# RWKV attention feeding a routed expert layer: the first chunks reordered, an early table and some weight splits moved

## The chip, the cores and the metric

The kernel runs on one core of a Trainium2 chip. The metric is the device time of one execution in microseconds (us), as the median of several runs. The core has five engines that each work through their own instructions in order: TensorE (PE, with its weight loads as PEld), VectorE (DVE), ScalarE (ACT), GpSimd (POOL) and SyncE (SP). SP here only issues transfers; ACT and POOL issue some as well. PE has two clock levels, 1.2 and 2.4 GHz; the profile gives the granted clock as a share of the higher one.

## The reference

Two stages follow each other. The first is a linear attention with a decaying state, for 4 batches, 8 heads, 768 positions and a head size of 48; the second sends each of the 3072 rows of its result to one of 8 experts.

```python
for t in range(S):
    kt, vt, rt = k[:, :, t], v[:, :, t], r[:, :, t]
    cur = np.einsum('bhd,bhe->bhde', u[None] * kt, vt)
    y[:, :, t] = np.einsum('bhd,bhde->bhe', rt, state + cur)
    state = w[None, :, :, None] * state + np.einsum('bhd,bhe->bhde', kt, vt)
...
logits = x @ w_gate                      # x: the attention's result, 3072 x 384
expert_idx = np.argmax(logits, axis=1)   # gate_w: softmax weight of that expert
...
h = np.maximum(np.einsum('ecd,edf->ecf', disp, w1), 0.0)   # 384 -> 1024
y = np.einsum('ecf,efd->ecd', h, w2)                       # 1024 -> 384
out[i] = gate_w[i] * y[expert_idx[i], pos[i]]
```

Each expert takes the rows sent to it in order, up to a capacity.

## The kernel before

**Chunks.** The attention is cut into 24 chunks of 128 positions (`NI`, six per batch). Chunk `i` reads four tensors: `dm` (r and k with the head dimension on partitions, 393 KB), `bd` (r, k and v compact per half chunk, 590 KB), and, unless it is the last of its batch, `tk` and `tv` (k and v rows, 197 KB each); together 1.38 MB. All are issued by SP, in `load` (L485) and `load_v` (L503). `dm`, `tk` and `tv` have three buffers each and `bd` has four, so a load waits until the chunk three or four back has been used.

**Work of a chunk.** POOL forms the bonus products r*u*k from `bd` and the table `ubt`, which holds u on all 128 partitions (`bonus`, L512 and L513). DVE sums them (`reduce_bonus`, L561). ACT writes the sums on diagonals of two score tiles `s0` and `s1` (`diag`, L520 and L521, eight instructions) and copies v into block form (`blocks`, L527). DVE scales r and k by powers of the decay (`prep_keys`, L537 and L545) and k rows by `kk` (`prep_values`, L554). PE multiplies these to scores (`scores`, L568 and L571). DVE and ACT lay the scores over the diagonals through the mask `msk` (`masks`, L580 to L582). PE forms the state's update (`update`, L592; DVE L600 and L602 add and scale it) and the chunk's values (`values`, L613, L614, L617). ACT copies them to `x` (L619, two buffers) and issues the store to DRAM (L620). One chunk later PE turns `x` round (`xpose`, L80; ACT copies it to `xt`, L82) and forms its eight logits (`logits`, L91; ACT L92 reads them out of the same PSUM tile that the next `xpose` takes).

**Order.** The order on every engine is the order of the source; nothing is rearranged. Ahead of the loop (L626 to L663) the first chunks are loaded and prepared: chunk 2 entirely, with its sum of the bonus, before the loop begins. In the loop, iteration `i` issues on PE: scores of chunk i+1, the transposition of x of i-1, the update of i, routing matmuls (`step`, L105), the values of i, the logits of i-1. `diag` of chunk i+2 stands after the values in iterations 0 and 1 and before them later. Preparation of chunk i+3 (`prep`) ends the iteration.

**Routing.** `route` (L110) is a generator that `step` advances by a stage: DVE finds the best expert, PE ranks the rows (L136, L137, into a PSUM tile with the tag `lg`, one buffer), DVE compares the ranks with a ramp, and PE adds the rows' numbers into a table (L180) which DVE accumulates in `acc` (L181). In iteration 20 the table is read a first time for expert 0 (`table`, L261: four transpositions into a tile with the tag `lg`, three DVE instructions). It is read for all experts after the last chunk's routing, and the rows are then gathered by indirect transfers of POOL (`gather`, L275).

**Weights.** `wstream` (L233) loads expert weights in pieces (SP, L239) and splits each of 14 halves into a high part (ACT, L247) and a low part (DVE, L248). `PLAN0` places the fetches and splits of expert 0 in the loop's iterations. After the loop `layer1(0, f)` for f = 0 to 7 runs the first layer of expert 0's early rows; the last chunk's routing is interleaved with it (L713 to L738).

**Start of the kernel.** POOL builds constants (the identity, `rev`, `eye`, the mask as float `mf`), DVE the powers of the decay (`setup1`), and PE runs matmuls on zeros (`warm`) so as to be busy. `ubt` is loaded by two broadcast transfers (L492). `setup3` (L446) builds the routing's constants on POOL.

## Time and profile before

| | us |
|---|---|
| median of three runs | 435.44 |
| lowest and highest | 433.3 and 436.03 |
| the profiled execution, whole | 437.47 |
| its span, first to last instruction | 435.7 |

| engine | busy us | share of the span |
|---|---|---|
| PE | 414.2 | 95% |
| DVE | 273.9 | 63% |
| POOL | 235.2 | 54% |
| ACT | 228.9 | 53% |

The mean granted clock of PE was 0.964. The attention takes the first 173 us or so; the experts take the rest. The shares are averages over stages with different limits, so each stage is read for itself. "Busy" of PE counts a matmul at the lower clock as twice as long, so a PE that is busy all the time may still be working at half its speed. A line "A <- B" of the waits says that A stood idle until B released it.

### The profile page before, as it was taken

The page shows a single profiled execution, that of the slowest core. Times are in us where ns is not written, and L with a number is a line of the kernel's source. Part 1 is how long each engine was busy: PE and PEld are TensorE (multiplying, and loading weights), DVE is VectorE, ACT ScalarE, POOL GpSimd, SP SyncE. Part 2 cuts the span into 40 slices and gives each one's busy share as a digit, 9 for nine tenths or more (in the row PEclk, how much of TensorE's full clock was granted, in tenths as well). Part 3 has the DMA queues.
Part 4 walks back from the last instruction along what each step waited for, and adds up shares of the span by engine and source line. Part 5 has one row for each costly group of instructions (what it writes and reads, how often), then busy time and mean ns, then how long its engine had stood idle before and what let it go on. Part 6 is the DMA issues. An engine that isn't in the chain of part 4 may idle for free.

```text
span 435.7 us, 8123 instructions
## 1 busy us (share of the span) xinstructions
PE 414.2 (95%) x2911; PEld 402.6 (92%) x2912; DVE 273.9 (63%) x595; ACT 228.9 (53%) x607; POOL 235.2 (54%) x242
## 2 busy tenths in 40 slices
PE   7789999999999799999999999999999999999993
PEld 3678999999999798899999999999999999999992
DVE  5696879999999957676355365464563554644310
ACT  6755787777778545354346265273472552742401
POOL 5985148387846351158886384682882540620703
PEclk9686999999999989699999999999999999999998
DMA  7996997789689113326736456566565553430112
GB/s 221 300 296 206 342 296 247 251 274 297 221 259 327 38 57 108 129 68 153 189 75 170 142 119 161 138 155 171 122 157 160 163 149 126 116 85 5 25 33 65
DMA packets 52963, 72.07 MB, mean 165 GB/s; under 512 B 29654, under 2 KB 38312, under 8 KB 52912
## 3 DMA queue, kind: packets, MB, share of 16 engines
q1 hardware_dynamic: 20528, 56.84, 42.5%
q0 software_dynamic: 28928, 9.89, 10.9%
q10 hardware_dynamic: 3456, 4.72, 3.0%
q8 instruction: 25, 0.41, 0.4%
q14 instruction: 26, 0.21, 0.2%
HBM read 62.06 MB, written 9.79 MB: 165 GB/s over the span
## 4 chain that ended last, share of the span: by engine, by line
PE 75%; DMA 8%; DVE 5%; issue 4%; POOL 3%; ACT 2%; SPq 1%; POOLq 0%; ACTq 0%; DVEq 0%
PE a L304 8%; PE a L305 8%; PE a L306 8%; PE b L323 7%; PE b L325 7%; PE b L324 7%; PE y L613 4%; PE y L614 4%; PE a L568 4%; PE y L617 4%; PE a L571 4%; DMA xg<-x_dr,idsc 3%; PE xp L91 3%; PE u L592 3%; PE yp L339 2%
## 5 line engine op out<-in xcount | busy, mean ns | idle before, releaser
L331 POOL DMA_INDIRECT out<-yo,idsc x28 | 59.3, 2116 | 63.0 <-ACT yo L330 56.6
L278 POOL DMA_INDIRECT xg<-x_dr,idsc x28 | 60.3, 2152 | 42.9 <-PE tp L287 35.9
L304 PE MATMUL a<-xh,ws 128*128 128x412 f32 (+2 forms) x216 | 76.7, 355 | 0.4 <-DVE hl L310 0.4
L309 ACT ACTIVATE hh<-a 128x412 fp32r<-128x412 f32 (+2 forms) x72 | 35.1, 487 | 74.8 <-PE a L306 74.5
L305 PE MATMUL a<-xl,ws 128*128 128x412 f32 (+2 forms) x216 | 73.3, 339 | 0.1
L306 PE MATMUL a<-xh,ws 128*128 128x412 f32 (+2 forms) x216 | 73.0, 338 | 0.0
L323 PE MATMUL b<-hh,ws 128*128 128x412 f32 (+2 forms) x216 | 72.8, 337 | 0.0
L324 PE MATMUL b<-hl,ws 128*128 128x412 f32 (+2 forms) x216 | 71.3, 330 | 0.0
L325 PE MATMUL b<-hh,ws 128*128 128x412 f32 (+2 forms) x216 | 71.3, 330 | 0.0
L310 DVE SCALAR_TENSOR_TENSOR hl<-a,hh 128x412 fp32r<-128x412 f32 (+2 forms) x72 | 39.5, 551 | 49.2 <-ACT hh L309 48.9
L248 DVE TENSOR_TENSOR ws<-wr,ws 128x384 fp32r<-128x384 f32 (+1 forms) x112 | 66.4, 612 | 3.7 <-ACT ws L247 3.6
L247 ACT CAST ws<-wr 128x384 fp32r<-128x384 f32 (+1 forms) x112 | 59.3, 557 | 0.1
L326 DVE COPY yt<-b 128x412 f32<-128x412 f32 (+2 forms) x27 | 14.5, 539 | 68.0 <-PE b L325 68.0
L304 PEld LDWEIGHTS a<-xh,ws 128*128 128x128 f32 x216 | 41.7, 193 | 1.0 <-DVE hl L310 0.6
L305 PEld LDWEIGHTS a<-xl,ws 128*128 128x128 f32 x216 | 41.7, 193 | 0.8 <-DVE xl L292 0.6
L306 PEld LDWEIGHTS a<-xh,ws 128*128 128x128 f32 x216 | 41.6, 192 | 0.1
L291 ACT CAST xh<-tp 128x412 fp32r<-128x412 f32 (+2 forms) x27 | 12.5, 478 | 54.1 <-PE tp L287 54.1
L324 PEld LDWEIGHTS b<-hl,ws 128*128 128x128 f32 x216 | 40.7, 189 | 0.1
L323 PEld LDWEIGHTS b<-hh,ws 128*128 128x128 f32 x216 | 40.7, 189 | 0.1
L325 PEld LDWEIGHTS b<-hh,ws 128*128 128x128 f32 x216 | 40.5, 188 | 0.1
L512 POOL TENSOR_TENSOR t<-bd,ubt 128x384 f32<-128x384 f32 x24 | 30.3, 1264 | 17.7 <-DMA bd<-bdc 11.9
L520 ACT ACTIVATE s<-eye,bon 128x64 f32<-128x64 f32 x96 | 32.4, 338 | 13.7 <-DVE bon L561 7.6
(191 smaller groups left out, 864.1 us busy)
## 6 DMA issues: line engine op xcount, KB each, us to landing
bd<-bdc SPq DMA_DIRECT2D x23, 576.0 KB, 5.6
wr<-w SPq DMA_DIRECT2D x24, 512.0 KB, 6.6
wr<-w SPq DMA_DIRECT2D x32, 384.0 KB, 7.2
dm<-dmj SPq DMA_DIRECT2D x24, 384.0 KB, 4.5
x_dr<-x ACTq DMA_DIRECT2D x24, 192.0 KB, 3.3
tk<-rkv SPq DMA_DIRECT2D x20, 192.0 KB, 5.7
tv<-rkv SPq DMA_DIRECT2D x20, 192.0 KB, 5.8
xg<-x_dr,idsc POOLq DMA_INDIRECT x28, 12.9
```

Of the source, the lines that this page charges most:

```text
L247: nc.scalar.copy(out=hi, in_=r)
L248: nc.vector.tensor_tensor(out=lo, in0=r, in1=hi.bitcast(F32), op=ALU.subtract)
L278: nc.gpsimd.indirect_dma_start(out=xg[k % 2][:q, i], out_offset=None, in_=x_dr[:n, :], in_offset=bass.IndirectOffsetOnAxis(ap=ids[k][:q, i ...
L304: nc.tensor.matmul(a, lhsT=wh, rhs=xh[:, d, :n], start=d == 0, stop=False)
L305: nc.tensor.matmul(a, lhsT=wh, rhs=xl[:, d, :n], start=False, stop=False)
L306: nc.tensor.matmul(a, lhsT=wl, rhs=xh[:, d, :n], start=False, stop=d == 2)
L309: nc.scalar.activation(hh[:, f, :n], a, AF.Relu)
L310: nc.vector.scalar_tensor_tensor(out=hl[:, f, :n], in0=a, scalar=0.0, in1=hh[:, f, :n].bitcast(F32), op0=ALU.max, op1=ALU.subtract)
L323: nc.tensor.matmul(o, lhsT=wh, rhs=hh[:, f, :n], start=f == 0, stop=False)
L324: nc.tensor.matmul(o, lhsT=wh, rhs=hl[:, f, :n], start=False, stop=False)
L325: nc.tensor.matmul(o, lhsT=wl, rhs=hh[:, f, :n], start=False, stop=f == 7)
L331: r = nc.gpsimd.indirect_dma_start(out=out[:, :], out_offset=bass.IndirectOffsetOnAxis(ap=ids[k][:qo, i, 0:1], axis=0), in_=yo, in_offset= ...
```

## The change

- **Loads.** `us` (u in two rows, 3 KB) replaces the two broadcasts into `ubt`: POOL builds a 2 x 128 matrix `half` of zeros and ones, PE multiplies it with `us`, ACT copies the result to `ubt`. Chunk 0's first part of `bd` is issued before `dm`; `bd`'s v part and `tv` of chunk 0 come before chunk 1; chunk 3 and `tv` of chunks 1 and 2 are issued before the work on chunk 0.
- **Masks and constants.** `msk` and the memset of `snb[0]` go ahead of the bonus products on POOL. `setup3` is split: its first part stands before the bonus of chunk 3, the rest (`setup4`) after the values of chunk 1. The zeroing of `vdb[2]` on ACT goes behind the masks of chunk 0.
- **Warm matmuls.** 8 in place of 10 at the start; 6 before the scores of chunk 0 in place of 3 after the transpositions of `setup1`. The matmul and copy of `setup_keys` go ahead of the scores of chunk 0.
- **Bonus sums.** Up to chunk 4 the sum is taken by itself: for chunks 2, 3 and 4 behind the values of chunks 0, 1 and 2, directly ahead of their `diag` (which for chunk 4 moves from before to after the values). `prep_values` of chunk 2 also moves there.
- **Stores.** The stores of x for chunks 0, 1 and 2 are issued by SP, not ACT.
- **Early table.** In iteration 20 the routing step and the values come before the table of expert 0, not behind it.
- **Splits.** Splits 11, 12 and 13 of expert 0 leave iterations 22 and 23 and follow `layer1(0, 2)`, `(0, 3)` and `(0, 4)`.

The diff, its core:

```diff
-SPLIT0 = {..., 21: (6, 7, 8), 22: (9, 10, 11), 23: (12, 13)}
-PLAN0 = [((FETCH0[i],) if i in FETCH0 else (), SPLIT0.get(i, ())) for i in range(NI)]
+SPLIT0 = {..., 21: (6, 7, 8), 22: (9, 10)}
+PLAN0 = [((FETCH0[i],) if i in FETCH0 else (), SPLIT0.get(i, ())) for i in range(NI)] + [((), (n,)) for n in range(11, 14)]
...
+            us = sup.tile([2, DM], F32, name="us")
+            half = sup.tile([2, 128], F32, name="half")
+            nc.sync.dma_start(out=us, in_=ub)
             make_identity(nc, idn)
+            nc.gpsimd.memset(half, 1.0)
+            nc.gpsimd.affine_select(out=half, in_=half, ...)
+            nc.gpsimd.affine_select(out=half, in_=half, ...)
...
-            warm(10)
+            warm(8)
+            up = ps1.tile([128, DM], F32, tag="lg", name="up")
+            nc.tensor.matmul(up, lhsT=half, rhs=us, start=True, stop=True)
...
+            nc.scalar.copy(out=ubt.rearrange("p a b d -> p (a b d)"), in_=up)
             setup2()
+            nc.gpsimd.tensor_copy(out=msk, in_=mf)
             for a in (rtb[1], kdb[1]):
                 nc.gpsimd.memset(a[96:], 0.0)
+            nc.gpsimd.memset(snb[0], 0.0)
...
-                if "bon" not in t:
+                if i > 4:
                     reduce_bonus(i)
...
-                nc.scalar.dma_start(out=x_dr[C * i:C * i + C, :], in_=x)
+                (nc.sync if i < 3 else nc.scalar).dma_start(out=x_dr[C * i:C * i + C, :], in_=x)
...
             load(0)
-            load(1)
             nc.sync.dma_start(out=T[0]["bd"][:, 2], in_=bdc[0, 0, :, 2])
             load_v(0)
+            load(1)
             load(2)
+            load_v(1)
+            load(3)
+            load_v(2)
             bonus(0)
...
             w128, oki, g = setup1(sup, ps1)
+            setup_keys(ps1, g)()
+            warm(6)
             prep_keys(0)
             scores(0)
-            keys = setup_keys(ps1, g)
+            blocks(0)
             reduce_bonus(0)
+            prep_values(0)
+            prep_keys(1)
             diag(0)
-            keys()
+            masks(0)
+            nc.scalar.copy(out=vdb[2].rearrange("p a e -> p (a e)"), in_=zc.broadcast_to([128, 768]))
             setup_state(sup, w128, oki)
-            blocks(0)
-            prep_keys(1)
-            masks(0)
-            prep_values(0)
             prep_values(1)
+            reduce_bonus(1)
             diag(1)
             blocks(1)
-            load_v(1)
-            load(3)
             bonus(2)
...
-            prep(2)
+            setup3()
             bonus(3)
-            setup3()
+            prep_keys(2)
...
             for i in range(NI):
-                each(load_v, i + 2)
+                if i != 1:
+                    each(load_v, max(i + 2, 3))
...
                 update(i)
+                if i < NI - 1:
+                    step()
+                if i > 2:
+                    each(diag, i + 2)
+                values(i)
                 if i == 20:
                     ids[0] = table("a", 0, PASSES[0][2], range(1), ("lg", 1))[:, 0]
-                if i < NI - 1:
-                    step()
-                if i > 1:
-                    each(diag, i + 2)
-                values(i)
                 if i == NI - 1:
                     step()
-                if i <= 1:
+                if i == 0:
+                    prep_values(2)
+                if i <= 2:
+                    reduce_bonus(i + 2)
                     diag(i + 2)
                 each(blocks, i + 2)
                 scale(i)
                 step()
+                if i == 1:
+                    setup4()
...
             for f in range(2, 5):
                 layer1(0, f)()
+                next(ws)
```

## Rows read from the trace of the kernel before

**Rows 1.** The page's 40 equal slices of the span, in tenths.
```profile
PEclk9686999999999989699999999999999999999998
```

**Rows 2.** Busy time by stretch: start:end, length, engines, granted clock, DMA share, GB/s.
```profile
10.00:15.00 5.00, 1.05 (x5) 1.08 (x6) 3.53 (x8) 3.14 (x12) 4.73 (x8) 0.71 1.05 315
...
30.00:35.00 5.00, 3.91 (x19) 3.67 (x19) 4.72 (x7) 3.37 (x12) 2.96 (x4) 0.50 1.03 305
```

**Rows 3.** The critical chain, 0 to 75 us: start, length, what.
```profile
3.00 5.99 DMA bd<-bdc
...
15.68 8.70 DMA dm<-dmj
...
24.46 0.38 ACTq L620
...
24.89 0.35 ACT s L520
...
26.91 0.40 ACT vd L527
...
41.23 0.99 PE a L568 x8
...
43.08 0.33 PE xp L80 x3
...
45.88 0.89 PE y L617 x8
46.77 0.60 PE xp L91 x6
47.37 0.99 PE a L568 x8
```

**Rows 4.** Waits from 5 to 41 us: total us, times, longest.
```profile
DVE bon L561 <- POOL t L513: 6.3, 3, 3.4
ACT s L520 <- DMA dm<-dmj: 5.8, 2, 3.6
...
PE xp L91 <- ACT xt L82: 1.6, 1, 1.6
```

**Rows 5.** Timeline of the first 30 us: start, length, instruction.
```profile
9.16 1.01 POOL L512 TENSOR_TENSOR t<-bd,ubt 128x384 f32<-128x384 f32 x1 [4.29 <-DMA bd<-bdc]
...
11.99 0.68 DVE L537 TENSOR_TENSOR rt<-dm,ft 96x512 f32<-96x512 f32 x1
...
12.59 1.22 DVE L545 TENSOR_TENSOR kd<-dm,kb 96x1024 f32<-96x1024 f32 x1
...
13.95 2.05 PE L568 MATMUL a<-rt,kd 128*128 128x128 f32 x8 [3.96 <-POOL msk L635]
...
20.59 1.08 PE L568 MATMUL a<-rt,kd 128*128 128x128 f32 x8
...
24.13 2.01 DVE L545 TENSOR_TENSOR kd<-dm,kb 96x1024 f32<-96x1024 f32 x1
...
29.57 2.06 PE L568 MATMUL a<-rt,kd 128*128 128x128 f32 x8
```

**Rows 6.** Timeline around iteration 20, 148 to 159 us.
```profile
151.06 0.18 PE L136 MATMUL rk<-oh,tri 128*128 128x16 bf16 x1 [2.56 <-DVE idsa L272]
...
158.21 0.44 DVE L581 COPY_PREDICATED s1b<-msk,a 128x256 f32<-128x256 int32 x1 [3.26 <-PE a L571]
```

**Rows 7.** Timeline after the last chunk, 174 to 187 us.
```profile
174.28 0.93 ACT L247 CAST ws<-wr 128x384 fp32r<-128x384 f32 x2
...
175.10 1.03 DVE L248 TENSOR_TENSOR ws<-wr,ws 128x384 fp32r<-128x384 f32 x2
...
186.91 0.42 DVE L310 SCALAR_TENSOR_TENSOR hl<-a,hh 128x256 fp32r<-128x256 f32 x1 [1.16 <-ACT hh L309]
```

**Rows 8.** Transfers issued from 0 to 50 us: count, KB each, median us to landing.
```profile
x_dr<-x ACTq DMA_DIRECT2D x4, 192.0 KB, 6.2
...
ubt<-ub SPq DMA_DIRECT2D x2, 96.0 KB, 4.5
```

More of the change, by code (lines that the diff above doesn't have):

```diff
@@ L31 @@
 FETCH0 = {3: 0, 4: 1, 9: 2, 13: 3, 16: 4, 18: 5, 19: 6}
[L32 to L33 removed]
+SPLIT0 = {7: (0,), 8: (1,), 10: (2,), 13: (3,), 15: (4,), 16: (5,), 21: (6, 7, 8), 22: (9, 10)}
+PLAN0 = [((FETCH0[i],) if i in FETCH0 else (), SPLIT0.get(i, ())) for i in range(NI)] + [((), (n,)) for n in range(11, 14)]
 GROUPS = [(0, 4), (4, 4), (8, 4), (12, 4), (16, 2), (18, 2), (20, 2), (22, 2)]
@@ L376, in rwkv_moe @@
             nc.sync.dma_start(out=wt, in_=wv)
+            us = sup.tile([2, DM], F32, name="us")
+            half = sup.tile([2, 128], F32, name="half")
+            nc.sync.dma_start(out=us, in_=ub)
             make_identity(nc, idn)
+            nc.gpsimd.memset(half, 1.0)
+            nc.gpsimd.affine_select(out=half, in_=half, compare_op=ALU.is_ge, fill=0.0, base=0,
+                                    pattern=[[1, 128]], channel_multiplier=-64)
+            nc.gpsimd.affine_select(out=half, in_=half, compare_op=ALU.is_ge, fill=0.0, base=63,
+                                    pattern=[[-1, 128]], channel_multiplier=64)
             nc.gpsimd.memset(hm, 1.0)
@@ L418, in setup1 @@
                 nc.scalar.copy(out=g, in_=gp)
-                nc.scalar.copy(out=vdb[2].rearrange("p a e -> p (a e)"), in_=zc.broadcast_to([128, 768]))
-                warm(3)
                 return sq[7], oki, g
@@ L452, in setup3, with setup4 @@
                 start(0)
+            def setup4():
                 nc.gpsimd.iota(ramp, pattern=[[1, WL]], base=0, channel_multiplier=0, allow_small_or_imprecise_dtypes=True)
@@ L487, in load @@
                 t = T[i] = {}
-                dm = t["dm"] = ld.tile([96, 2, NP, 128], F32, tag="dm", name=f"dm{i}", bufs=3)
-                nc.sync.dma_start(out=dm, in_=dmj[b, c])
-                if i == 0:
-                    for h in range(2):
-                        nc.sync.dma_start(out=ubt[64 * h:64 * h + 64].rearrange("p a b d -> p (a b d)"),
-                                          in_=ub[h:h + 1].broadcast_to([64, NP * 2 * D]))
                 bd = t["bd"] = ld.tile([128, 3, 8, D], F32, tag="bd", name=f"bd{i}", bufs=4)
@@ L496, in load @@
                     nc.sync.dma_start(out=bd[:, 0:2], in_=bdc[b, c, :, 0:2])
-                else:
+                dm = t["dm"] = ld.tile([96, 2, NP, 128], F32, tag="dm", name=f"dm{i}", bufs=3)
+                nc.sync.dma_start(out=dm, in_=dmj[b, c])
+                if i:
                     nc.sync.dma_start(out=bd, in_=bdc[b, c])
@@ L633, in rwkv_moe @@
                 nc.gpsimd.memset(a[96:], 0.0)
-            nc.gpsimd.memset(snb[0], 0.0)
-            nc.gpsimd.tensor_copy(out=msk, in_=mf)
             bonus(1)
             w128, oki, g = setup1(sup, ps1)
+            setup_keys(ps1, g)()
+            warm(6)
             prep_keys(0)
             scores(0)
-            keys = setup_keys(ps1, g)
+            blocks(0)
             reduce_bonus(0)
+            prep_values(0)
+            prep_keys(1)
             diag(0)
-            keys()
+            masks(0)
+            nc.scalar.copy(out=vdb[2].rearrange("p a e -> p (a e)"), in_=zc.broadcast_to([128, 768]))
             setup_state(sup, w128, oki)
-            blocks(0)
-            prep_keys(1)
-            masks(0)
-            prep_values(0)
             prep_values(1)
+            reduce_bonus(1)
             diag(1)
             blocks(1)
-            load_v(1)
-            load(3)
             bonus(2)
```

1 line of the change is left out of this document (removed).

## The prediction

> **What bounds the kernel now.** I read the page's slices first. The granted clock is well below full in three places: slices 2 to 4, slice 15 and slice 17 [rows 1]; at 10.9 us a slice these are the stretch from 11 to 44 us, that from 152 and that from 174 us. Elsewhere PE runs at 2.4 GHz and is busy nearly all the time, so a gain is to be looked for in these three places, and the change touches all three.
>
> The critical chain comes next. From 41.23 us on it is PE, one loop iteration after another; iteration 3 lasts 47.37 − 41.23 = 6.14 us [rows 3]. Before that it is transfers and short steps of other engines: chunk 0's `bd` lands at 3.00 + 5.99 = 8.99 us [rows 3] and the bonus starts at 9.16 [rows 5]; a load of `dm` lands at 15.68 + 8.70 = 24.38 us and releases a store's issue on ACT [rows 3]. By the timeline, the scores that open iterations 0, 1 and 2 start at 13.95, 20.59 and 29.57 us [rows 5], those of iteration 3 at about 41.2 [rows 3]. So iterations 0 to 2 took 6.6, 9.0 and 11.6 us where 6.14 (4.3 for the first) would do. The windows say why a longer one costs twice: transfers run at 300 GB/s with all engines taken, and from 30 to 35 us PE gets half its clock [rows 2]; matmuls of L568 that take 1.08 us there take 2.06 [rows 5].
>
> The waits name what is late: DVE waited 6.3 us in three places for POOL's bonus, and with DVE's strict order the masks behind it waited too; ACT stood 5.8 us in two places before `diag` until a transfer landed, which was the issue of a store; PE waited 1.6 us for `xt` and 4.0 us for `msk` or the keys beside it [rows 4, 5].
>
> **The change, part by part: the head.** I rebuild the opening from rows.
>
> *Loads.* A chunk is 1.38 MB, at 300 GB/s 4.6 us, below the 6.14 us of an iteration; the head's transfers bind only because they start late and in the wrong order. The two `ubt` transfers (4.5 us to landing [rows 8]) become 3 KB, and `bd` has nothing ahead of it, so it lands 2 to 4 us before 8.99. POOL then sets the bonus's start: it gets `half` (three small instructions, some 0.7 us), `msk` and a memset (0.6 and 0.5) ahead of it and was free at 9.16 − 4.29 = 4.9 us, hence about 6.8 us against 9.16 [rows 5]. With two instructions of 1.01 us and DVE's sum the first `diag` starts near 9.5. By bytes ahead of it, `dm` of chunk 1 lands at about 10 us, of chunk 2 at 13.8, of chunk 3 at 18.4, of chunk 4 at 23.
>
> *Iteration 0.* Keys take 0.68 + 1.22 us of DVE [rows 5], so the scores of chunk 1 start at about 12.2, not 13.95. The six warm matmuls and `gq` delay the scores of chunk 0 to about 10.3; they end at 12.2, just in time. `diag` takes 26.91 − 24.89 = 2.0 us [rows 3] and ends at 12.5, two masks at 13.4, ahead of the values at 14.7. PE's work of iteration 0 is 6.14 − 0.33 − 0.89 − 0.60 = 4.3 us (no transposition, no state, no logits [rows 3]): it ends at 16.6, and the keys of chunk 2 (13.8 + 1.9, behind chunk 1's sum) are ready at 16.3.
>
> *Iteration 1.* 6.14 us, and a wait: `xt` of chunk 0 stands on ACT behind `diag` and `blocks` of chunk 2, 3 us that start when POOL's bonus is summed, at 19.0; the logits wait 0.8 us. It ends at 23.6.
>
> *Iteration 2.* The next `xpose` needs the logits read out by ACT, behind `diag` and `blocks` of chunk 3: with DVE's sum at 24.4 this is 27.5 us, and PE, through its scores at 25.5, waits 2.0 us. It ends at 31.8. *Iteration 3* has this wait once more, as `diag` of chunk 4 now follows the values: 3.1 us of ACT plus a copy against 2.5 us of PE, 1.2 us. It ends at 31.8 + 6.14 + 1.2 = 39.1 us, against 47.37 [rows 3]: 8.3 us gained at the full clock with nobody in anybody's way.
>
> Two deductions. DVE and POOL slow each other: the keys' instruction takes 1.22 us, and 2.01 when POOL works beside it [rows 5]. Iterations 0 to 2 hold three of these and some smaller ones; bounds 0 and 4 us, I take 1.5. And PE still has gaps ahead of 12 us. In the profile a gap of 3.96 us [rows 5] stands just before the clock falls, so one stretch at 1.2 GHz is likely; it doubled 1.08 us to 2.06. Bounds 0 (no fall) and 5 us (a whole iteration, 11.6 − 6.14, as iteration 2 was); I take 1.8. **The head gives 8.3 − 1.5 − 1.8 = 5.0 us**, bounds 0 and 8.3.
>
> *Stores by SP.* ACT no longer holds still for the store's turn (5.8 us [rows 4]); this gain is in the sum already. Behind each store on SP stand the later loads: of `dm`, `bd` and `tk` for chunks 6 and 7 and `tv` of chunk 4. They wait for buffers until about then anyway, and are used two iterations later. The Trainium skill speaks against this part: in "DMA: Bandwidth & Descriptors", section "Issuing engines are not separate DMA queues", it says that transfers run on the same 16 engines whoever starts them, and that a choice of issuer only saves the sequencer's time. By that rule two moved issues give 2 x 0.38 us. The rows show more than issue time at stake on ACT, since what is behind the issue waits as well; that the landing gets no earlier is a rival below.
>
> *Covered.* `setup4` (some 1.7 us of POOL) goes behind chunk 1's values, under POOL's idle time between bonuses; uncovered it delays one bonus by 1.7 us. The zeroing of `vdb[2]` (0.8 us of ACT) stands where ACT waits for the sum of chunk 1. The `up` matmul runs in place of two warm ones; its copy delays `kb` by 0.5 us, under the wait for `dm`.
>
> **The early table.** In iteration 20 the rank matmul waits 2.56 us, as the table's tile has the same tag and is read by DVE behind two state updates [rows 6]. PE then falls to 1.2 GHz for a while (slice 15 [rows 1]). Afterwards the rank needs no such read, and the values (1.8 + 0.89 us [rows 3]) run while DVE works off its backlog; table and DVE reads meet about 3 us later with nothing behind them. PE gains up to 2.6 us of waiting and about 1.7 us of half clock. DVE limits this: it then waited 3.26 us for the scores of chunk 22 [rows 6], and the masks behind them can move up by no more than that. I take 3.0, bounds 0 and 4.
>
> **The splits.** Splits 12 and 13 are 0.93 us of ACT and 1.03 us of DVE, between the last logits and the operands of `layer1(0, 0)` [rows 7]; without them these come about 0.5 us sooner. Afterwards three splits, 1.5 us of DVE, stand among `layer1`, where DVE had one idle piece of 1.16 us [rows 7]; the rest, 0.4, delays the accumulation for the last table. Two weight fetches wait for their buffers some 8 us longer, still ahead of their own splits. Net 0.5, bounds −0.5 and 3.5, the last if PE's fall to 1.2 GHz at about 176 us (slice 17 [rows 1]) goes too.
>
> **Sum.** 5.0 + 3.0 + 0.5 = 8.5 us. The profiled execution took 437.47 us (span 435.7), two more than the median of 435.44; from the median it is 435.44 − 8.5 = 427 us.
>
> **Rivals.**
>
> *PE keeps its full clock.* Then the head gives near its 8.3, the table 3 to 4 and the end 2 to 3: about 14 us, 421 us. For it: the new warm matmuls bridge the gap before chunk 0's scores. Against it: waits for ACT of 1 to 2 us remain in iterations 1 to 3.
>
> *The head stays slow.* ACT, DVE and POOL are near full there (POOL 4.73 of 5 us in one window [rows 2]), and if each iteration again ends in a wait that costs the clock, the head gains 0 to 1 us. With table and splits: 435.44 − 4 = 431.5 us.
>
> *The table's move does nothing.* If DVE, not the tile, holds iteration 20, the wait reappears at the next masks. Then 435.44 − 5.5 = 430 us.
>
> *The stores hold `x`; slower.* `x` has two buffers, so the copy of chunk 2's values waits until chunk 0's store has landed. By the rule above SP makes that no sooner: the median is 6.2 us [rows 8], and with loads ahead of it on the queue I put it at 31 us, just when the copy is ready. Each us later holds ACT, with `diag` of chunk 4 and the logits' copy behind it, and so PE; the stores of chunks 1 and 2 may repeat it. It takes 8.5 us in all to eat the gain and 13 to be slower by over 1%, three holds of over 4 us: with two of 6.2 and one of 1.5 about 441 us.
>
> **How the numbers follow.** The forecast, 424 to 429.5 us, gets 0.52; full clock 0.20; no table 0.10; slow head 0.12; stores 0.06. About 1% (4.4 us) is what a measurement of this kernel tells from no change: faster means below 431.1. Forecast, full clock, 0.06 of the no-table case and 0.02 of the slow head are faster, 0.80; the rest of these two, 0.14, the same; the stores 0.06, slower. The range from 420.5 to 432 leaves out the stores and the ends of the two outer cases.
>
> **What would show it.** In the new profile: the loads of `dm` for chunk 1 landing near 10 us; scores starting at about 12, 17, 24 and 33 us; no wait of ACT's `diag` for a transfer; iteration 20 without a wait of the rank for the table, and no fall of the clock at its place. Wrong would be: ACT's copy of `x` (L619) waiting for a transfer, DVE's keys at 2 us each, or slices of the clock below 8 tenths beyond the fourth.

## The result, and the profile after

The changed kernel takes 430.82 us as the median of 18 runs (427.8 to 433.56); the kernel before takes 435.94 us beside it (431.8 to 440.76, 18 runs). That is 5.1 us less by the medians; the ratio is 0.9915 [0.9887, 0.9943], a gain of 3.7 us. A ratio leaves out executions that lie over 1.5% above the fastest of their kernel and a median does not, so the two differ, by up to 2.4 us in the table of the experiments; I compare parts by medians on the same chip and give the ratio where it says something else. The forecast of 427.0 us was too low by 3.8: sign and range held, the size did not, and by the ratio the change lies just inside the 1% that I had given 0.14.

The page of the changed kernel, its span, its engines and the granted clock in 40 slices:

```profile
span 428.3 us, 8132 instructions
...
PE 408.5 (95%) x2914; PEld 394.9 (92%) x2915; DVE 275.0 (64%) x595; ACT 229.3 (54%) x608; POOL 237.0 (55%) x245
...
PEclk9998999999999999999999999999999999999998
```

Of the three places where the clock was low [rows 1], the ones at iteration 20 and at the start of the first layer are gone, and one slice of the head is left, at 8 tenths (the first slice deceives, see the head below). The two profiled executions stand 437.47 − 430.09 = 7.4 us apart, more than the medians, since that of before lay 1.5 us above its median. The trace splits the 7.4 by events on PE: the scores of chunk 7 start at 58.80 before and 57.32 after, 1.5 us of **head**; iteration 20, from the scores of chunk 21 to those of chunk 22, lasts 156.10 − 145.16 = 10.94 us before and 150.27 − 143.68 = 6.59 after, 4.35 us of **table**; from chunk 22 to the second layer's first matmul it is 34.81 us before and 32.87 after, 1.9 us at the **end**, where the splits are (the rest of the span gives 0.4 back). So between these two profiles the table gave more than forecast, the end more, and the head, the largest term, far less.

**Iteration 20.** Timeline of the kernel after, 146 to 153 us (start, length, instruction, idle time before and its releaser):

```profile
146.60 0.17 PE L136 MATMUL rk<-oh,tri 128*128 128x16 bf16 x1
...
149.38 0.42 PE L267 MATMUL tba<-idn,acc 72*64 72x72 f32 x4
...
150.27 1.14 PE L577 MATMUL a<-rt,kd 128*128 128x128 f32 x8
...
152.98 0.42 DVE L590 COPY_PREDICATED s1b<-msk,a 128x256 f32<-128x256 int32 x1
```

The rank no longer waits [rows 6 has 2.56 us], the table's transpositions follow without a wait, and the masks of chunk 22 stand 5.2 us sooner, with no wait of DVE ahead of them.

**The head.** Opening scores of each chunk on PE, in us; the forecast is that of the steps ahead of their deductions.

| chunk | forecast | before | after | after, a second profile (`e14_again`) | the same head alone (`e1_head`) |
|---|---|---|---|---|---|
| 1 | 12.2 | 13.95 | 14.82 | 13.89 | 14.94 |
| 2 | 16.6 | 20.59 | 19.83 | 18.47 | 19.84 |
| 3 | 23.6 | 29.57 | 27.70 | 28.12 | 27.70 |
| 4 | 31.8 | 41.08 | 38.01 | 36.13 | 36.41 |
| 5 | 39.1 | 47.22 | 45.68 | 43.81 | 44.09 |

Already the first row is wrong: chunk 1 came hardly sooner than before, or later. Timeline of the kernel after, 4 to 34 us:

```profile
7.10 1.51 POOL L521 TENSOR_TENSOR t<-bd,ubt 128x384 f32<-128x384 f32 x1 [0.46 <-ACT ubt L488]
8.69 1.32 POOL L522 TENSOR_TENSOR t<-t,bd 128x384 f32<-128x384 f32 x1
...
7.85 2.71 DVE L550 TENSOR_TENSOR kd<-dm,kb 96x512 f32<-96x512 f32 x2
10.49 0.54 DVE L570 TENSOR_REDUCE bon<-t 128x8 f32<-128x384 f32 x1
...
12.37 2.02 DVE L554 TENSOR_TENSOR kd<-dm,kb 96x1024 f32<-96x1024 f32 x1
...
10.53 2.70 PE L477 MATMUL warm<-oob 128*128 128x512 bf16 x6
13.07 1.05 PE L577 MATMUL a<-rt,kd 128*128 128x128 f32 x8
...
27.01 0.83 PE L91 MATMUL xp<-wgs,xt 128*128 128x8 f32 x6 [1.43 <-ACT xt L82]
...
32.02 0.55 PE L80 MATMUL xp<-idn,x 128*128 128x128 f32 x3 [2.32 <-ACT l L92]
```

The bonus starts at 7.10 (6.8 forecast) instead of 9.16 [rows 5]. What sets chunk 1's scores is PE itself: it goes without a break from the six warm matmuls to the scores of chunk 0, at 13.07 and not at 10.3 us, and from these to the scores of chunk 1. The warm matmuls run at 1.2 GHz and take 2.70 us; in `e15_stores`, at 2.4 GHz, the same six take 1.46 (timeline of that run, 8 to 12 us):

```profile
8.96 1.46 PE L478 MATMUL warm<-oob 128*128 128x512 bf16 x6
```

The clock record of the changed kernel's profile begins with the rise at 13.03 us, and views print full clock for what lies ahead of the first record; the 9 of its first slice and the 1.00 of the window from 10 us below are no evidence against these durations.

A second limit lies close behind. DVE now forms the keys while POOL forms the bonus: chunk 0's take 2.71 us (1.28 before), POOL's two products 1.51 and 1.32 instead of 1.01 and 0.99, and chunk 1's keys take 2.02 instead of 1.22, ending at 14.39, 0.4 us ahead of the scores that use them. Chunk 2's keys, 2.01 us, end at 17.67 + 2.01 = 19.68, just before its scores at 19.83. What ACT costs later is as forecast: the waits of PE from 5 to 46 us (us in total, times, longest) have 3.6 us for the logits' read where I had 2.0 + 1.2.

```profile
POOL t L521 <- DMA bd<-bdc: 3.9, 4, 1.7
...
PE xp L80 <- ACT l L92: 3.6, 2, 2.3
...
ACT s L529 <- DVE bon L570: 3.4, 2, 1.9
...
PE xp L91 <- ACT xt L82: 1.4, 1, 1.4
```

No line of ACT waiting for a transfer is left [rows 4 has 5.8 us]. The windows (start:end, length, busy time of PE, PEld, DVE, ACT, POOL, granted clock, DMA share, GB/s) show one fall of the clock after the first rise, from 33.5 to 36.9 us, behind PE's wait of 2.32 us, in the stretch that [rows 2] shows at 0.50:

```profile
10.00:15.00 5.00, 5.00 (x26) 3.07 (x25) 4.12 (x5) 3.42 (x11) 4.35 (x5) 1.00 1.01 318
30.00:35.00 5.00, 2.98 (x22) 2.98 (x23) 3.49 (x8) 2.69 (x9) 2.05 (x3) 0.85 1.05 317
```

### The profile page after: what moved, and what is told of

It reads as the page before. It is cut to its first block, busy times and chain, and to the rows that moved or that the text cites. A ratio compares the mean times of both kernels' runs of the same rounds, so it can differ in the third digit from the quotient of the medians.

```text
span 428.3 us, 8132 instructions
## 1 busy us (share of the span) xinstructions
PE 408.5 (95%) x2914; PEld 394.9 (92%) x2915; DVE 275.0 (64%) x595; ACT 229.3 (54%) x608; POOL 237.0 (55%) x245
## 4 chain that ended last, share of the span: by engine, by line
PE 68%; DVE 13%; issue 6%; ACT 4%; POOL 4%; DMA 4%; POOLq 0%; ACTq 0%; DVEq 0%
PE a L305 7%; PE a L304 7%; PE a L306 7%; PE b L323 7%; PE b L325 7%; PE b L324 7%; DMA xg<-x_dr,idsc 4%; PE y L623 3%; PE y L622 3%; PE y L626 3%; PE a L577 3%; PE a L580 2%; PE yp L339 2%; POOL xg L278 2%; PE tp L287 2%
## 5 line engine op out<-in xcount | busy, mean ns | idle before, releaser
L304 PE MATMUL a<-xh,ws 128*128 128x412 f32 (+2 forms) x216 | 75.5, 350 | 0.8 <-DVE hl L310 0.8
L305 PE MATMUL a<-xl,ws 128*128 128x412 f32 (+2 forms) x216 | 72.4, 335 | 0.1
L306 PE MATMUL a<-xh,ws 128*128 128x412 f32 (+2 forms) x216 | 72.1, 334 | 0.0
L304 PEld LDWEIGHTS a<-xh,ws 128*128 128x128 f32 x216 | 40.7, 188 | 1.3 <-DVE hl L310 1.0
L305 PEld LDWEIGHTS a<-xl,ws 128*128 128x128 f32 x216 | 40.7, 189 | 0.8 <-DVE xl L292 0.6
L306 PEld LDWEIGHTS a<-xh,ws 128*128 128x128 f32 x216 | 40.6, 188 | 0.1
L622 PE MATMUL y<-vd,s 128*128 128x96 f32 x192 | 37.9, 280 | 0.0
```

Of the source, the lines that this page charges most:

```text
L304: nc.tensor.matmul(a, lhsT=wh, rhs=xh[:, d, :n], start=d == 0, stop=False)
L305: nc.tensor.matmul(a, lhsT=wh, rhs=xl[:, d, :n], start=False, stop=False)
L306: nc.tensor.matmul(a, lhsT=wl, rhs=xh[:, d, :n], start=False, stop=d == 2)
L622: nc.tensor.matmul(y[:, p, 0:96], lhsT=t["s0"][:, p], rhs=t["vd"][:, 2 * p], start=p == 0, stop=False)
```

## The experiments

The theory after the result: the table's term was too small and the head's too large; the head is held by several limits of nearly one length, so that taking one away uncovers the next. The rivals are one cause that holds all of it: the clock ahead of 13 us, the order on ACT, the logits' wait, POOL beside DVE, or the stores.

| run | median | before, same chip | difference | ratio [95%] |
|---|---|---|---|---|
| `e1_head` | 434.74 | 435.87 | −1.1 | 0.9919 [0.9875, 0.9962] |
| `e2_table` | 431.28 | 435.87 | −4.6 | 0.9897 [0.9863, 0.993] |
| `e3_splits` | 434.85 | 435.87 | −1.0 | 0.9967 [0.9934, 1.0] |
| `e4_actstore` | 431.93 | 435.87 | −3.9 | 0.992 [0.9884, 0.9956] |
| `e5_warmfill` | 429.23 | 433.35 | −4.1 | 0.9938 [0.9905, 0.9972] |
| `e6_actorder` | 429.07 | 433.35 | −4.3 | 0.9921 [0.9879, 0.9962] |
| `e7_logits` | 426.45 | 433.35 | −6.9 | 0.9896 [0.9832, 0.9961] |
| `e9_halfbonus` | 428.95 | 433.35 | −4.4 | 0.9945 [0.9909, 0.9981] |
| `e10_wgs` | 428.78 | 432.96 | −4.2 | 0.9941 [0.9903, 0.9978] |
| `e11_front` | 427.65 | 432.96 | −5.3 | 0.9911 [0.9876, 0.9945] |
| `e12_wgslogits` | 426.03 | 432.96 | −6.9 | 0.9888 [0.9827, 0.9949] |
| `e13_all` | 424.83 | 432.96 | −8.1 | 0.9837 [0.9783, 0.989] |
| `e14_again` | 430.33 | 435.12 | −4.8 | 0.9897 [0.9839, 0.9955] |
| `e15_stores` | 424.24 | 435.12 | −10.9 | 0.977 [0.9709, 0.9831] |
| `e16_diag4` | 429.71 | 435.12 | −5.4 | 0.9889 [0.9829, 0.995] |

`e7_logits` and `e12_wgslogits` to `e16_diag4` have six runs each, the others ten or twelve.

### The three parts alone: `e2_table`, `e3_splits`, `e1_head`

`e2_table` is the kernel before with the table's move only:

```diff
                 update(i)
-                if i == 20:
-                    ids[0] = table("a", 0, PASSES[0][2], range(1), ("lg", 1))[:, 0]
...
                 values(i)
+                if i == 20:
+                    ids[0] = table("a", 0, PASSES[0][2], range(1), ("lg", 1))[:, 0]
```

> The kernel before with only the early table moved behind the values of chunk 20. Theory 1: the wait of 2.56 us of the rank matmul and the 3.4 us at 1.2 GHz behind it go, 3 to 4.3 us less: 431.6 to 433 against 435.9. Theory 2 (DVE, not the tile, holds iteration 20): the wait reappears at the next masks or at the table itself, and the time stays within 1 us of before.

4.6 us, most of the whole gain. The rank of its trace has no wait any more (timeline of this kernel, 146 to 150 us):

```profile
146.47 0.17 PE L136 MATMUL rk<-oh,tri 128*128 128x16 bf16 x1
149.25 0.42 PE L267 MATMUL tba<-idn,acc 72*64 72x72 f32 x4
```

Its page has the clock of before in the head and none of the later falls, the one in slice 17 included, though its splits are those of before:

```profile
PEclk9687999999999999999999999999999999999998
```

`e3_splits` is the kernel before with the splits only:

```diff
-SPLIT0 = {..., 21: (6, 7, 8), 22: (9, 10, 11), 23: (12, 13)}
-PLAN0 = [... for i in range(NI)]
+SPLIT0 = {..., 21: (6, 7, 8), 22: (9, 10)}
+PLAN0 = [... for i in range(NI)] + [((), (n,)) for n in range(11, 14)]
...
                 layer1(0, f)()
+                next(ws)
```

> The kernel before with only splits 11, 12 and 13 of expert 0 moved into the early first layer. Theory 1 (forecast): 0.5 us less, 435.4. Theory 2: the profiles show the layer starting 6.1 us earlier and the second layer 7.8 us earlier, and PE at 2.4 GHz where it was at 1.2 from 175.9 to 182.7 us before; if the splits did this, 2 to 3 us less, 433 to 434. Theory 3: DVE among the layer's pieces becomes late for the last table, 0.5 to 1 us more.

1.0 us, with an interval that touches no change at all. Its trace keeps the wait of the rank (timeline, 147 to 152 us):

```profile
150.74 0.18 PE L136 MATMUL rk<-oh,tri 128*128 128x16 bf16 x1 [2.55 <-DVE idsa L272]
```

But the clock does not fall behind it here, and iteration 20 lasts 154.15 − 144.85 = 9.30 us, against 6.59 without the wait and 10.94 with wait and fall: of the table's 4.35 us, 2.7 are the wait and 1.6 the clock. The end, from chunk 22 to the second layer's first matmul, takes 33.72 us here with the new splits and 32.65 in `e2_table` with the old ones, both without a fall, so no trace shows a gain of the splits.

`e1_head` is the changed kernel with both of these put back, that is, the head alone.

> The changed kernel with the early table and the three splits put back where the kernel before had them: the head alone. In the profiles the opening scores of iteration 5 (chunk 6) came 1.5 us earlier than before (51.88 against 53.36), so theory 1, that the head as it stands saves only about 1.5 us and the table and the end the rest, expects 434.0 to 435 against 435.9 of before. Theory 2, that the profiled execution of before was merely a lucky one in the head and the head saves the 5 us forecast, expects about 431. If the head saves nothing, 436.

1.1 us by the medians, 3.5 [1.7, 5.4] by the ratio. Its twelve runs fall into two clumps, seven at 430.6 to 435.5 and five at 438.2 to 442.4. Its trace has the old wait (timeline, 147 to 149 us):

```profile
147.98 0.18 PE L136 MATMUL rk<-oh,tri 128*128 128x16 bf16 x1 [2.56 <-DVE idsa L272]
```

Behind it the clock falls for 6.8 us, in slice 15 of its page; slice 17 is high here too:

```profile
PEclk9999999999999979999999999999999999999998
```

The kernels with this wait scatter widely (before: 431.8 to 440.8), that with the table's move alone does not (429.7 to 433.5). The parts sum to 6.7 us where the whole gives 4.8 and 5.1; by the medians the head is worth from −0.8 (whole less the other two) to 1.1 us, and the ratio alone puts it higher. The traces lie between: chunk 7 opens at 57.32, 55.44 and 55.72 us in three profiles of the new head (after, `e14_again`, `e1_head`) and at 58.80, 57.18 and 58.46 in three of the old one (before, `e2_table`, `e3_splits`), 2.0 us apart on average.

### Single causes in the head: `e4_actstore`, `e5_warmfill`, `e6_actorder`, `e9_halfbonus`

All are edits of the changed kernel. `e4_actstore` puts the stores back on ACT (`nc.scalar.dma_start` for every chunk):

> The changed kernel with the stores of x of chunks 0, 1 and 2 issued by ACT again. Theory 1: ACT again stands still until an earlier transfer has landed, 2 to 3 us each for the first two stores, diag of the next chunk behind it is late, and with it the opening scores of iterations 2 to 4: 2 to 4 us slower than the changed kernel, 433 to 435. Theory 2 (only the issue time counts, 0.34 us each): within 0.7 us of the changed kernel's 430.8.

About 1 us worse than the change by the median, and not at all by the ratio (0.992 beside 0.9915). The mechanism is there: `x` of chunk 0 is ready at 20.72, ACT issues its store at 25.38, and `diag`, whose sum had been ready since 22.2, stands behind it (timeline, 20 to 26 us):

```profile
20.23 0.49 ACT L628 COPY x<-y 128x384 f32<-128x384 f32 x1
...
25.38 0.38 ACTq L629 DMA_DIRECT2D x_dr<-x  x1
```

PE's logits then wait for another thing (waits from 14 to 50 us):

```profile
PE xp L91 <- DMA wgs<-wg: 5.0, 1, 5.0
```

The gate's weights `wgs`, 12 KB, were not in my rows at all. Their load stands on SP behind the loads of chunk 4.

`e5_warmfill` gives PE work in the two gaps ahead of 9 us:

```diff
                 nc.scalar.copy(out=g, in_=gp)
+                warm(3)
...
             nc.tensor.matmul(up, lhsT=half, rhs=us, start=True, stop=True)
+            warm(2)
```

> The changed kernel with two more warm matmuls behind the u product and three behind the transpositions of setup1, where PE stood idle 1.79 us: a PE that is busy without a break from 1.3 us on. Theory 1 (PE late: it had 1.2 GHz until 13.03 us, so the scores of chunk 0 came at 13.07 and all of ACT's work behind their masks with them): the higher clock comes by 10 us, scores of chunk 0 at 11 to 11.5 us, scores of chunk 2 at 18 to 18.5 and not 19.83, 1 to 2 us less in all, 429 to 430. Theory 2 (DVE's keys, drawn out to 2 us each beside POOL, are what is late): scores of chunks 1 and 2 no earlier than their keys, 14.4 and 19.7 us; within 0.7 us of the changed kernel's 430.8.

No gain (−4.1 against −4.8 and −5.1). Chunk 2 opens at 19.0 us, but the unchanged kernel shows both 18.47 and 19.83, so that earlier start proves nothing; chunk 3 opens at 30.83, later than after, because the logits wait 4.8 us. The waits put this down to an instruction of ACT that had long ended; the `wgs` load, issued at 19.4, took 10.0 us to land, and 29.4 is when the logits run.

`e6_actorder` moves `masks(0)` behind the zeroing of `vdb[2]` and `setup_state`:

> The changed kernel with the zeroing of vdb[2] and the state's decay tile (0.7 and 0.8 us of ACT) ahead of the masks of chunk 0, where ACT waits 1.73 us for the scores, not behind them. Theory 1 (ACT's order behind chunk 0's scores sets the pace): diag of chunk 1 starts at 16.5 us and not 17.66, masks of chunk 1 and scores of chunk 3 1 us earlier (26.7 against 27.70), about 1 us less, 429.8. Theory 2 (DVE's keys): no change beyond 0.5 us.

No gain either. The logits wait 3.4 us for `wgs`, and the view of that tile gives its time from issue to landing:

```profile
DMA to landing us min/median/max: 10.3/10.3/10.3
```

`e9_halfbonus` leaves out POOL's second product for chunks 0 to 3, so the bonus there lacks the factor k:

```diff
-                nc.gpsimd.tensor_tensor(out=t1, in0=t1, in1=t["bd"][:, 1], op=ALU.mult)
+                if i > 3:
+                    nc.gpsimd.tensor_tensor(out=t1, in0=t1, in1=t["bd"][:, 1], op=ALU.mult)
```

> The changed kernel without POOL's second product of the bonus for chunks 0 to 3 (the factor k is left out there), which takes about half of POOL's work beside DVE in the head. Theory 2 (DVE and POOL in each other's way): the keys of chunks 0, 1 and 2 take 1.2 to 1.6 us and not 2.0 to 2.7, scores of chunk 2 at 18 to 18.8 us and not 19.83; 1 to 2 us less. Theory 1 (PE's clock and ACT's order): scores of chunk 0 still at 13.1, of chunk 2 at 19.3 or later, less than 0.5 us gained in all.

With POOL's second products gone, the time is the same. The keys get shorter in part (timeline; 1.91, 2.02 and 1.22 us where after had 2.71, 2.02 and 2.01):

```profile
7.17 1.91 DVE L551 TENSOR_TENSOR kd<-dm,kb 96x512 f32<-96x512 f32 x2
...
12.51 2.02 DVE L555 TENSOR_TENSOR kd<-dm,kb 96x1024 f32<-96x1024 f32 x1
...
16.42 1.22 DVE L555 TENSOR_TENSOR kd<-dm,kb 96x1024 f32<-96x1024 f32 x1
```

Chunk 7 opens at 56.77, 0.55 us sooner than after, which proves nothing, as two profiles of the unchanged kernel lie 1.9 us apart there (57.32 and 55.44). Chunk 1's keys, which still take 2.02 us, run beside other work of POOL (`prep_values` of chunk 1), so the run takes away a part of the overlap only. It shows that the second products do not hold the head, and leaves open what POOL beside DVE costs in all.

### The changed kernel again, and the waits around the logits: `e14_again`, `e10_wgs`, `e7_logits`, `e12_wgslogits`

> The changed kernel once more, on the chip that runs the other two: all theories expect it 4 to 5 us under the kernel before; it is the mark for what follows, and its trace shows whether the three waits of the head (logits for xt or wgs, and twice the transposition for the logits' read) stand in another execution too: 1 to 3 us, 2.2 us and 1.3 us.

The second profile of the same kernel takes another way through the head: the clock rises sooner, and it is `wgs` that PE waits for, not `xt` (timeline):

```profile
17.28 0.33 SPq L671 DMA_DIRECT2D wgs<-wg  x1
...
27.45 0.81 PE L91 MATMUL xp<-wgs,xt 128*128 128x8 f32 x6 [2.81 <-DMA wgs<-wg]
...
31.32 0.90 PE L80 MATMUL xp<-idn,x 128*128 128x128 f32 x3 [0.19 <-ACT l L92]
...
39.45 0.55 PE L80 MATMUL xp<-idn,x 128*128 128x128 f32 x3 [1.31 <-ACT l L92]
```

Behind the wait for `wgs` the clock falls, from 28.9 to 32.3 us; the wait for the logits' read is then 0.19 us in iteration 2 and 1.31 in iteration 3.

`e10_wgs` issues that load behind those of chunk 2 instead of chunk 4:

```diff
             load(2)
+            nc.sync.dma_start(out=wgs, in_=wg)
...
             load(4)
-            nc.sync.dma_start(out=wgs, in_=wg)
```

> The changed kernel with one line moved: the load of the gate weights wgs (12 KB) is issued behind the loads of chunk 2, not behind those of chunk 4. Theory 3 (the logits of chunk 0, in iteration 1, can't begin before wgs has landed, at 24 to 29.4 us in the runs so far, whatever comes earlier ahead of them): in executions where wgs was late they begin at 27 us and not at 29.5, when xt is there; scores of chunk 3 never later than 28 us; 0 to 2 us less than the changed kernel. Theory 1 (only ACT's order and PE's clock count): within 0.5 us of it.

The wait for `wgs` is gone from the trace, and the time is not better (−4.2): PE waits 3.5 us in two places for the logits' read and 1.1 for `xt` instead. `e7_logits` takes away the next one: in iterations 1 and 2 the logits go ahead of the bonus sum, `diag` and `blocks` of chunk i+2, so that ACT reads them out before these.

```diff
+                if 1 <= i <= 2:
+                    logits(i - 1, xt, wk, sm, ps1, "tbl")
                 if i <= 2:
                     reduce_bonus(i + 2)
...
                 if i >= 1:
-                    logits(i - 1, xt, wk, sm, ps1, "tbl")
+                    if i > 2:
+                        logits(i - 1, xt, wk, sm, ps1, "tbl")
```

> The changed kernel with the logits of chunks 0 and 1 issued ahead of the bonus sum, diag and blocks in iterations 1 and 2, so that ACT reads them out of PSUM before its 3 us of diag and blocks. Theory 1 (ACT's order: PE waits 2.32 us and 1.31 us for that read, and falls to 1.2 GHz behind it): both waits go, iteration 2 lasts about 7 us and not 10.3, iteration 3 6.2 and not 7.7; 3 to 5 us less, 426 to 428. Theory 2 (the work behind is late anyway, as diag of chunk 3 and its masks come no sooner): the wait reappears at the masks or at the values; within 1 us of 430.8.

−6.9 us, the only single edit whose median gains on the change, by about 2 us; its ratio, 0.9896, is no better than that of the change beside `e14_again`, 0.9897 (the kernels of its own chip, below, say more). The wait for the read falls from 3.6 to 1.2 us. Iteration 2, the one that took 10.31 us after, takes 34.35 − 28.21 = 6.14 us, as one in the steady state [rows 3]; timeline, 28 to 35 us:

```profile
28.21 1.14 PE L577 MATMUL a<-rt,kd 128*128 128x128 f32 x8
...
34.35 1.14 PE L577 MATMUL a<-rt,kd 128*128 128x128 f32 x8
```

`e12_wgslogits` has both edits:

> wgs early as in e10, with the order of e7 (logits of chunks 0 and 1 ahead of diag and blocks). In e7 wgs had landed at 23.6 us in its profile and PE waited for xt instead; so theory 3 expects no more than e7 in a profile, but fewer slow executions: 3 to 5 us less than the changed kernel, scores of chunk 4 at 34.5 us as in e7 against 38.01.

−6.9 again: by the times, the early `wgs` adds nothing to `e7_logits`, though chunk 7 opens 2.3 us sooner in its profile (51.22 against 53.50).

### `diag` of chunk 4: `e16_diag4`

The bonus sum and `diag` of chunk 4 go back ahead of the values (three bounds in the source lower by one).

> The changed kernel with one part undone: bonus sum and diag of chunk 4 stand again where they were, the sum in the preparation of chunk 4 and diag ahead of the values of chunk 2. Theory 1 (the 1.31 us that PE waits in iteration 3 is a cost of this part): the wait goes and the time is 1 to 1.3 us under the changed kernel's. Theory 2 (the sum, now earlier on DVE, holds the masks of chunk 3, as POOL's bonus of chunk 4 is late): the wait moves to iteration 2, which lasts longer than 10.3 us; no gain or 1 us lost.

The wait in iteration 3 goes, as expected (38.68 to 44.82 is 6.14 us), but that of iteration 2 grows:

```profile
PE xp L80 <- ACT l L92: 3.1, 1, 3.1
```

0.6 us less than the change beside it: not to be told apart. The wait moved.

### Several at once: `e11_front`, `e13_all`, `e15_stores`

`e11_front` is `e5_warmfill`, `e6_actorder` and `e10_wgs` together; `e13_all` adds `e7_logits` to it.

> wgs early as in e10, with the warm matmuls of e5 and ACT's order of e6. Theory 3 says that e5 and e6 brought the chunks ahead of the logits forward by 0.8 to 1.3 us and lost it to wgs (PE waited 4.8 and 3.4 us there); without that wait scores of chunk 3 start at 25 to 26.5 us against 27.70, and the end is 1.5 to 3 us earlier than that of the changed kernel. Theory 1 alone expects about 1 us; if DVE's keys hold the pace, nothing (scores of chunk 2 at 19.5 or later).

> wgs early, the warm matmuls of e5, ACT's order of e6 and the logits of e7 together. If the waits for wgs, for xt behind ACT's late diag and for the logits' read are what the head lost, they add up: scores of chunk 3 at 25 to 26.5 us, of chunk 4 at 31 to 33, of chunk 7 at 51 to 53 against 57.32, 5 to 7 us less than the changed kernel. If transfers or DVE take over as the bound, no better than e12.

−5.3 and −8.1. The kernels of one chip set the edits beside each other. The logits' order gains wherever it is added: `e7_logits` is 2.7 us below `e5_warmfill`, `e6_actorder` and `e9_halfbonus` taken together (426.45 against a median of 429.18), `e12_wgslogits` 2.8 below `e10_wgs`, `e13_all` 2.8 below `e11_front`. The warm matmuls and ACT's order, which showed nothing alone, go with 1.1 us (`e11_front` against `e10_wgs`) and 1.2 us (`e13_all` against `e12_wgslogits`), within the scatter of these runs. The trace of `e13_all` shows the next limit, from 38 to 43 us (timeline):

```profile
40.32 0.39 ACTq L631 DMA_DIRECT2D x_dr<-x  x1
...
40.74 1.03 ACT L538 COPY vd<-bd 64x384 f32<-64x384 f32 x2 [2.20 <-DMA bd<-bdc]
...
42.02 0.90 PE L80 MATMUL xp<-idn,x 128*128 128x128 f32 x3 [2.66 <-ACT l L92]
```

Chunk 3's `x` is copied at 38.09 + 0.46 = 38.55, but its store leaves ACT only at 40.32, just after an earlier load of `bd` landed at 40.24; `blocks` and the logits' read stand behind it, and PE waits 2.66 us. It is what [rows 3] show before: a store of ACT leaving at 24.46 when a `dm` load landed at 24.38. The trace names the reason: the transfers that SP and ACT issue count on eight semaphores in turn, and an issue waits until the last transfer on its own semaphore, the eighth before it, has landed. For the store of 40.32 that is the `bd` load issued at 31.35, for the one of 24.46 the `dm` load issued at 15.68. `e15_stores` issues the stores of chunks 3 to 5 from SP too:

```diff
-                (nc.sync if i < 3 else nc.scalar).dma_start(out=x_dr[C * i:C * i + C, :], in_=x)
+                (nc.sync if i < 6 else nc.scalar).dma_start(out=x_dr[C * i:C * i + C, :], in_=x)
```

> The version of e13 with the stores of chunks 3, 4 and 5 issued by SP as well. In e13 ACT stood 2.2 us behind chunk 3's store, until a load had landed at 40.24 us, and PE 2.66 us behind that. Theory 1 (the issue holds ACT): both waits go, scores of chunk 7 at 51 us and not 53.36, 1 to 2.5 us less than e13. Theory 2 (the transfers are the bound by now: 300 GB/s, ACT waits for bd itself): the wait moves to blocks or to the copy of x, and the time stays within 0.7 us of e13.

424.24 us against 435.12, ratio 0.977 [0.9709, 0.9831], and 6.1 us below the changed kernel beside it: faster than both kernels. Over `e13_all` itself the gain is less sure: 2.8 us by the differences, 0.6 by the two medians, and the intervals overlap; in the profiles chunk 7 opens 4.3 us sooner (53.36 to 49.06). In its page no slice ahead of the last is low:

```profile
PEclk9999999999999999999999999999999999999998
```

`e12_wgslogits` prints the same line with a fall of 3.4 us at 8.9 us, which two slices share and round away; in `e15_stores` the record itself has no fall between the rise at 4.50 us and 417 us. Its window shows PE busy throughout the stretch that [rows 2] has at half clock:

```profile
30.00:35.00 5.00, 5.00 (x48) 4.96 (x48) 4.97 (x8) 3.87 (x14) 3.86 (x3) 1.00 1.06 286
```

Chunk 7 opens at 49.06 us in this profile (its fastest execution, 421.85), 9.7 sooner than before: more than the 8.3 that I had computed as the head's ideal. What the edits of the front, `wgs`, the logits and the stores each give in this kernel was not taken apart further.

How full the head is by then is shown by one window over the first 50 us (same columns). The kernel before:

```profile
0.00:50.00 50.00, 40.90 (x273) 36.25 (x275) 36.19 (x74) 31.44 (x93) 32.29 (x87) 0.83 0.89 265
```

The kernel after:

```profile
0.00:50.00 50.00, 41.22 (x289) 34.49 (x291) 38.44 (x77) 33.08 (x100) 34.64 (x90) 0.97 0.91 270
```

And `e15_stores`:

```profile
0.00:50.00 50.00, 45.72 (x368) 40.36 (x370) 46.05 (x91) 39.39 (x119) 38.77 (x93) 1.00 0.99 306
```

DVE is busy 46 of 50 us in the last one, 36 in the first, and the transfers' share rises from 0.89 to 0.99. That is where its next limit must be looked for; no run here tries it.

## Why the prediction was right or wrong

**What bounds the kernel: right in the main.** The head and iteration 20, two of the three stretches of low clock, gave time; the fall after the last chunk went without the splits too (below). A fourth stretch was not in the rows: ahead of its first rise PE ran at 1.2 GHz, until 5.23 us before and 13.03 after, and the page prints that as full clock.

**The head, 5.0 us: wrong, the step that failed.** It was worth between −0.8 and 1.1 us by the medians, 3.5 by the ratio of `e1_head`, 1.5 and 3.4 in the two profiles of the change. Of the 8.3 us I had deducted 1.5 for DVE beside POOL and 1.8 for one stretch of low clock, 3.3 in all; chunk 5 opened 6.6 and 4.7 us later than the steps had it (45.68 and 43.81 for 39.1).

*Iteration 0* failed first. Of the 12.2 us for chunk 1's scores, the bonus's start was right within 0.3, but two durations were wrong. The one that decided is PE's: the scores of chunk 0 were put at 10.3 us with the warm matmuls at full clock, and came at 13.07 and 12.13, with chunk 1's behind them without a break. Where the first rise came at 4.34 and 4.50 us, in `e13_all` and `e15_stores`, they came at 10.18 and 10.25. So low clock ahead of 13 us was not in the steps, and it took up the one stretch that I had deducted. The other duration is that of the keys, taken from instructions that had run alone: chunks 0 and 1 lost 1.4 + 0.8 = 2.2 us in the first profile and 0.8 in the second, chunk 2's another 0.8 in both (2.01 and 2.03 for 1.21). They are the next limit: in `e15_stores` chunk 1's keys end at 11.51 + 2.02 = 13.53 and its scores start at 13.68. I had named the effect with its row (2.01 against 1.22 [rows 5]), and "DVE's keys at 2 us each" as a sign of being wrong, and left it out of the steps that it decides: an edit that makes POOL start sooner puts it beside the keys. The Trainium skill, "SBUF — State Buffer", section "SBUF: two separate sides", says that VectorE, in instructions with two SBUF inputs, and GpSimd share a port pair that one of them holds for a whole instruction while the other stands. The trace agrees in size (0.80 and 1.43 us lost beside POOL products of about 1.0); POOL's products lengthened too, by 0.3 to 0.9 us.

*Iteration 1* was to take 7.0 us and took 7.87 and 9.65. The wait of 0.8 for `xt` was 1.43 in the one profile; in the other it was 2.81 for `wgs`, a load of 12 KB that I had not put on SP's queue. *Iteration 2* was to take 8.2 and took 10.31 and 8.01. In the first profile its wait for the logits' read was 2.32 (2.0 forecast), and the clock fell behind it for 3.4 us; `e1_head`, with the same head, has the wait (2.34) without the fall and takes 36.41 − 27.70 = 8.71, so the wait was forecast well and the fall cost 1.6. In the second profile the wait was 0.19, and the 3.4 us of low clock stood behind the wait for `wgs`. Each profile thus has two stretches of low clock where one was deducted. *Iteration 3* was right: 7.67 and 7.68 for 7.3, with a wait of 1.31 for 1.2.

So the waits that I had computed were there, and of nearly the right length. What the sum lacked is the second stretch of low clock, the lengthened keys and `wgs`. And the limits lie close together: `e10_wgs` and `e16_diag4` each remove one, and the next takes its place. Only the logits' order gains by itself; it removes the wait behind which the clock fell in the first profile.

**The stores by SP: partly right.** ACT's 5.8 us went [rows 4], and `e4_actstore` shows the old mechanism, but it is worth about 1 us at most as long as `wgs` and the logits' read hold PE anyway. In `e13_all`, where `wgs` does not, three more stores on SP go with a further 0.6 to 2.8 us. By the rule weighed in the prediction, from "DMA: Bandwidth & Descriptors" of the Trainium skill ("Issuing engines are not separate DMA queues"), they would give, as an estimate, 3 x 0.39 us of issuing. The trace of `e13_all` shows what that leaves out: the issue stands 1.8 us on ACT's queue with other work behind it.

**The table, 3.0 us: mis-sized.** The mechanism is right in each part: no wait, no fall of the clock. It measured 4.35 us in the profile and 4.6 by the median of `e2_table`, just past the upper bound of 4. The limit that I set by DVE's idle 3.26 us [rows 6] failed: even the masks came 5.23 − 1.48 = 3.75 us sooner once the head's part is taken off, and PE does not follow them one for one. The sum of PE's wait and its half clock, 2.6 + 1.7 = 4.3, was the right estimate; `e3_splits` shows the two apart, as 2.7 and 1.6.

**The splits, 0.5 us: not shown.** `e3_splits` has 1.0 us by the medians, with an interval that touches none, and its trace has no gain at the end. The end of the profiled execution gained 1.9 us, as the fall at 176 us [rows 1] did not return. I had that only as a bound and as the splits' doing; but that fall is gone from the pages of `e1_head` and `e2_table` too, which have the old splits, so it is not shown to be theirs.

**The rivals.** *The head stays slow* gave 431.5 us and comes nearest in time (430.8; the case without the table, 430 us, is as near, but the table's move worked), and also in kind, since iterations 1 to 3 do end in waits; I gave it 0.12, with its row, POOL busy 4.73 of 5 us [rows 2], in hand, and should have given it more. Full clock did not come in the changed kernel; `e15_stores` shows what it looks like. *The stores hold `x`* did not occur after; ACT's copy of `x` waits for a store once in `e13_all`, for 1.9 us, and once in `e11_front`, for 4.7, and neither kernel is slower than the changed one.

**Open.** Why the three parts sum to 6.7 us (9.4 by the ratios) and the whole gives 4.8 to 5.1 (3.7 to 4.5), and so what the head alone is worth; whether the runs of kernels with the table's wait scatter because the clock falls behind it in some executions (before and `e1_head` in the profiles) and not in others (`e3_splits`); what POOL beside DVE costs in all; how much the stores of chunks 3 to 5 give by themselves; and what decides when the clock rises ahead of 13 us.

## What to carry to other kernels

A stretch in which four engines and the transfers are all near full has many limits of one length: rebuild it with the durations that instructions have beside each other, and expect of one removed wait only its distance to the next. A trace after each edit says which to take next; whether edits that show nothing alone gain together, the scatter here leaves open. Look for what a queue served in order holds behind a long item: a small load behind large ones, a small read-out behind `diag`, a store's issue ahead of compute work; a wait that lets PE's clock fall is worth more than its length (4.35 us for one of 2.56). Where a clock record begins only at the first rise, read the level ahead of it from durations.

## What of the hardware was not expected

- The load of 12 KB among large ones took 6.3 to 10.3 us to land over the runs (8.8 before), about as long as the 8.70 us of a `dm` load [rows 3]; the 1.5 KB of `wt`, the first transfer of the kernel before, took 1.7 us. This suggests that what stands around a load counts more than its size; no run varied the size.
- An issue waited on its engine until an earlier transfer had landed, though its own data were ready: 24.46 after 24.38 before, 40.32 after 40.24 in `e13_all`. The transfer is the last one on the same semaphore, of eight used in turn.
- Two profiles of one kernel differ in the clock at the start: 1.2 GHz until 13.03 us in one (by the durations of its matmuls), 1.2 GHz from 8.4 to 11.8 us, after a rise at 5.0, in the other; each later step moves with it.
- The same wait of TensorE, 2.55 to 2.56 us, was followed by a fall of its clock in two profiles (before, `e1_head`) and not in a third (`e3_splits`).
